# A planned kernel: another price for GpSimd and VectorE at work together, ScalarE allowed to normalise, and two raw float32 tiles instead of four

## The chip, the core and the metric

The kernel runs on one core of one Trainium2 chip. Five engines of that core work in parallel, each through its own instructions in their order: TensorE (PE, matrix products; PEld is its weight load), VectorE (DVE), ScalarE (ACT), GpSimd (POOL) and SyncE (SP, which issues transfers). The metric is the time of one execution in microseconds; the median of the runs counts.

## What is computed

Three stages in a row, float32 in and out (setup and checks left out):

```python
# window attention: batch 2, 8 heads, 576 positions, 64 wide; only the 128 positions up to the own one count
scores = q @ k.T / 8 - slope[head] * distance          # masked outside the window
attn = exp(scores - max); attn = attn / (sum(attn) + 1e-9)
x = (attn @ v).reshape(1152, 512)
# four experts, each token weighted by p = probs / (sum(probs) + 1e-9)
x = sum over e of p[:, e] * (relu(x @ w1[e]) @ w2[e])   # 512 -> 1024 -> 512
# one wide layer
h = relu(x @ w_in); out = (h * h) @ w_out               # 512 -> 2048 -> 512
```

## The kernel before

A float32 product costs TensorE several passes. So the kernel splits an operand into a rounded part and a rest, both in the type float32r, and adds three products: high by high, high by rest, rest by high. Names ending in h hold rounded parts (`qh`, `xh`, `wh`), those ending in l the rests (`ql`, `xl`, `wl`). Rounding runs on ScalarE or VectorE (`rounded`, L519 and L521), the rest is a subtraction on GpSimd or VectorE (`rest`, L525). For a few early tiles the operand is taken raw, as float32, and nothing has to be split: those of the attention's first rows, and in the first expert, for the first 256 tokens, as many of the eight f tiles (128 columns of w1 each) as `RAW1` and `RAW2` say: four for the first product (g1, matmuls `hps<-xfirst,wraw`, L1819) and four for the second (g2, `yacc<-wraw,hfirst`, L1770). Raw inputs are the tiles `xfirst` and `wraw`.

The first part of the program, some 120 us, is not written in an order. Attention and the first expert's work on the first 768 tokens are handed as tasks to a list planner (`Plan`), with the engines that may run each, an estimate of how long it takes, what it waits for, and a due time. `run` takes at each step the task that can start first, or one with an earlier due time that starts within 0.15 us on the same engine, and writes its instructions. That alone sets the order on every engine; the hardware then runs each engine's list strictly in that order. Before, the planner charges for one collision: a VectorE task marked `shared` (roundings and rests out of SBUF) that starts while GpSimd is busy is charged up to twice its length more. A GpSimd task pays nothing.

An attention job is one tile of 128 queries (64 in the last tile) of one head pair. Its steps: `sc` scores on TensorE (L868, L852) from `qh`, `ql` and `khl` (rounded and rest of k), `jo` and `mx` on VectorE (mask, bias and row maximum, L886 and L906), `ex` on ScalarE (exp, L915), `in` on VectorE (one over the row sum, L922 and L926), `no` (multiply the rows by it, `norm`), `tp` on TensorE (transpose, L948, output `tp`, input `ts`), `hi` (copy to `pt`), `ow` and `be` on GpSimd (mask, L969), and for two pairs together `pv` on TensorE (L767, output `xps`). For all but the first rows `no` runs on GpSimd alone, two instructions (one for a tile of 64): L937, `ts<-ts,st`. Jobs are named here by pair and tile in order: A0, A1, B0, B1, C0 and so on. Each TensorE list holds jobs and f tiles mixed; f2 stands for tile 2 of the first product, g2.1 for tile 1 of the second.

Weights of the first expert come in eight pieces (`order`, i = 0 to 7: even for w1, odd for w2, two f tiles each). A piece that is not raw must be split before its first use. A raw piece is split later, for the other tokens. `parted` sets the order of the tasks, `room_` adds waits so that buffers are free. After the planner's part the rest (about 520 us) is written in a fixed order.

Of the kernel before, what the change touches and what calls it, by code (L numbers as in the profile page):

```python
# [12 lines left out]
ACTF = mybir.ActivationFunctionType  # L13
# [24 lines left out]
class Plan:  # L38
# [6 lines left out]
    OTHER = 0.3  # L45
    COLD = 3.0
    WARM = 24.0

    def __init__(self, slots):
        self.tasks = []  # L50
        self.slots = slots
        self.held = {k: [] for k in slots}
        self.at = dict(PE=0.0, ACT=0.0, DVE=0.0, POOL=0.0, SP=0.0)
        self.pool_busy = (0.0, 0.0)

    def add(
        self, name, opts, fn, deps=(), takes=(), bufs=(), due=0.0, follow=(), cold=True,
# [33 lines left out]
    def run(self, until=None):  # L91
        todo = self.tasks
        while todo and not (until and until()):
            cand = []
            for t in todo:
                r = self.ready(t)
                if r is None:
                    continue
                best = None
                for eng, occ, lat in t["opts"]:  # L100
                    start = max(self.at[eng], r)
                    if eng == "PE" and t["cold"] and start < self.COLD:
                        occ, lat = 1.7 * occ, lat + 0.7 * occ
                    if best is None or start + lat + self.OTHER < best[1] + best[3]:
                        best = (eng, start, occ, lat)
                cand.append((best, t))
            assert cand, [t["name"] for t in todo[:20]]
            first, _ = min(cand, key=lambda c: c[0][1])
            eng, start = first[0], first[1]
            (eng, start, occ, lat), t = min(  # L110
                (c for c in cand if c[0][0] == eng and c[0][1] <= start + self.LOOK),
                key=lambda c: c[1]["due"],
            )
            if eng == "DVE" and t["shared"] and self.pool_busy[1] > start:
                more = min(2.0 * occ, self.pool_busy[1] - start)
                occ, lat = occ + more, lat + more
            t["start"], t["end"] = start, start + lat
            self.gap = start - self.at[eng] if start < self.WARM else 0.0
            self.at[eng] = start + occ
            if eng == "POOL":  # L120
                self.pool_busy = (start, start + occ)
            for b in t["takes"]:
                self.held[b.kind].append(b)
            t["fn"](eng)
            for b in t["bufs"]:
                b.users -= 1
                b.end = max(b.end, t["end"])
            todo.remove(t)
# [3 lines left out]
def kernel(  # L132
# [14 lines left out]
    nc = tc.nc  # L147
# [12 lines left out]
    FTQ = FT // NQ  # L160
# [370 lines left out]
    def dve(n, lat=0.05):  # L531
        return ("DVE", 0.15 + 0.00105 * n, 0.15 + 0.00105 * n + lat)
# [289 lines left out]
    def job_tasks(u, i, t, add, b_, end, ready, G, q0, k0, pos, wide):  # L822
# [5 lines left out]
        raw = t == 0  # L828
# [4 lines left out]
        rows, squares = (2 * n, 1) if twin else (n, G)  # L833
        s = {k: Buf(k) for k in ("sc", "ts", "st", "tp")}
        m = n if raw else P
# [5 lines left out]
        def stage(name, opts, fn, lag, **kw):  # L841
            mine[name] = add(key + name, opts, fn, due=end - lag - later, follow=[last.get(name)], **kw)
            return mine[name]
# [84 lines left out]
        def norm(eng):  # L928
            ts, st = s["ts"].tile, s["st"].tile
            if eng == "DVE":  # L930
                nc.vector.tensor_tensor(
                    out=ts[0:rows], in0=ts[0:rows],
                    in1=st[0:rows, 3, 0:squares].unsqueeze(2).to_broadcast([rows, squares, m]), op=ALU.mult,
                )
                return
            for g in range(squares):
                nc.gpsimd.tensor_scalar(  # L937
                    out=ts[0:rows, g, :], in0=ts[0:rows, g, :], scalar1=st[0:rows, 3, g:g + 1],
                    scalar2=1.0, op0=ALU.mult, op1=ALU.mult,
                )  # L940
# [34 lines left out]
        if twin:  # L975
            if "last" not in task:
                task["last"] = plan.add(
                    "last", [("POOL", 2.2, 2.3)], build_last, due=70.0,
                    deps=[task["bias", x, False] for x in range(NP)],
                )  # L980
            tb.append(task["last"])
        us = G * (0.25 if raw else 2 * max(0.107, w * 0.00047))
        tsc = stage("sc", [pe(us)], scores, 7.4, deps=ready,
                    takes=[s["sc"]],
                    bufs=[b_[k] for k in (() if raw else ("qh", "ql", "khl"))])
        if not raw:
            us = 0.15 + 0.00105 * G * n
            tsc = stage("jo", [("DVE", us, us + 0.05)], join, 6.8, deps=[tsc, tb[-1] if twin else t_keep], bufs=[s["sc"]])
        us = G * (0.215 if raw else 0.16 + 0.001 * m)
        tmx = stage("mx", [("DVE", us, us + 0.1)], top, 9.5 if raw else 6.4,  # L990
                    deps=[tsc] + tb, takes=[s["ts"], s["st"]], bufs=[s["sc"]])
# [1 line left out]
                    7.5 if raw else 5.3, deps=[tmx], bufs=[s["ts"], s["st"]])  # L993
        tin = stage("in", [("DVE", 0.33, 0.38)], inv, 3.8, deps=[tex], bufs=[s["st"]])
        us = squares * (0.44 if raw else 0.24 + 0.00085 * m)
        tno = stage("no", [("POOL", us, us + 0.05)] + [dve(G * m)] * raw,
                    norm, 3.4, deps=[tin], bufs=[s["ts"], s["st"]])
        ttp = stage("tp", [pe(squares * 0.108)], turn, 2.4, deps=[tno, task["ident"]],
                    takes=[s["tp"]], bufs=[s["ts"]])
        thi = stage("hi", [act(G * n), dve(G * n)], hi, 2.0, deps=[ttp],  # L1000
# [665 lines left out]

    T0, T1, ITEM = 24.0, 34.0, 4.2

    RAW1, RAW2 = 4, 4

    wtask = {}

# [13 lines left out]
    def weight_parts(i):  # L1686
# [28 lines left out]
        room_ = [task["pv", NP - 1]] if j else []  # L1715
        if j > 1:
            room_ += [wtask["lo", parted[j - 2], 1], wtask.get(("used", parted[j - 2]))]
        if raw and j > PER - (RAW1 + RAW2) // FTQ:
            room_ += [itask["g2", FT - 1]] + [task["evl", u] for u in range(NP)]
        for h in range(2):  # L1720
            a = wtask["hi", i, h] = plan.add(
# [288 lines left out]
```

## Time and profile before

| | us |
|---|---|
| median of 3 runs | 647.51 (647.49 to 647.77) |
| the profiled execution | 648.88 |
| its span, first to last instruction | 646.9 |
| TensorE busy in it | 636.7 (98%) |
| VectorE, GpSimd, ScalarE busy | 467.4 (72%), 393.0 (61%), 295.4 (46%) |
| mean granted clock of TensorE | 0.997 |

The profiled execution took 1.37 us more than the median; 1.98 us of it lie around its span. In a timeline row the first number is the start in microseconds, the second the duration, and a bracket at the end gives the idle time before it and what ended it. Durations of neighbouring matmuls overlap, so a stretch is measured from start to start. "Busy" includes short matmuls on a tile `idle` that are there to occupy TensorE in the first microseconds.

### The profile page before, as it was taken

The numbers are of one execution on the slowest core, as the hardware profiler recorded it, in microseconds if no ns is written. First come the engines' busy times: TensorE is split into PE (matmuls) and PEld (weight loads), VectorE is DVE, ScalarE is ACT, GpSimd is POOL, SyncE is SP. The second block draws the span as 40 slices with busy tenths as digits, with TensorE's granted clock in tenths as the row PEclk, the third lists the DMA queues.
The fourth block names the chain that finished last, engine by engine and source line by source line (L and its number), as shares of the span: only waits on it lengthen the run. The fifth ranks groups of instructions, "written<-read, shape, count | busy, mean of one in ns | idle before, by whom it ended". The sixth has DMA issues, their size and how long they took to land.

```text
span 646.9 us, 11077 instructions
## 1 busy us (share of the span) xinstructions
PE 636.7 (98%) x3929; PEld 570.4 (88%) x3929; DVE 467.4 (72%) x1019; ACT 295.4 (46%) x744; POOL 393.0 (61%) x520
## 2 busy tenths in 40 slices
PE   9999999999999999999999999999999999999997
PEld 8767888899889999899899899899989899898996
DVE  6867967358887877876876876857777667767553
ACT  6867855334444444434434344346554543343230
POOL 2698977339784564565556546247786685665521
PEclk9989999999999999999999999999999999999999
DMA  9953341124125254354443443421114223001012
GB/s 231 275 144 84 81 106 47 39 93 131 34 65 163 82 143 151 93 157 126 119 142 114 130 131 115 130 83 66 33 41 157 81 83 114 16 2 50 1 65 82
DMA packets 46983, 64.70 MB, mean 100 GB/s; under 512 B 6480, under 2 KB 29264, under 8 KB 46928
## 3 DMA queue, kind: packets, MB, share of 16 engines
q1 hardware_dynamic: 35520, 39.48, 20.8%
q10 hardware_dynamic: 11408, 24.51, 12.9%
q8 instruction: 31, 0.51, 0.3%
q14 instruction: 24, 0.20, 0.1%
HBM read 53.23 MB, written 10.75 MB: 99 GB/s over the span
## 4 chain that ended last, share of the span: by engine, by line
PE 94%; POOL 3%; ACT 1%; issue 1%; DMA 0%; DVE 0%; POOLq 0%
PE yacc L1241 38%; PE hps L1150 35%; PE hps L1031 6%; PE yacc L1267 6%; PE sc L868 2%; PE xps L767 1%; PE tp L948 1%; PE hps L1819 1%; POOL ts L937 1%; PE sc L549 1%; POOL pt L969 1%; PE yacc L1770 1%; PE xtp L1333 1%; POOL ql L525 1%; ACT ts L915 0%
## 5 line engine op out<-in xcount | busy, mean ns | idle before, releaser
L1241 PE MATMUL yacc<-wh,hmem 128*128 128x512 f32 x716 | 227.8, 390 | 0.0
L1241 PEld LDWEIGHTS yacc<-wh,hmem 128*128 128x128 f32 x716 | 134.4, 188 | 27.1
L1241 PE MATMUL yacc<-wl,hmem 128*128 128x512 f32 x358 | 139.6, 390 | 0.0
L525 POOL TENSOR_TENSOR wl<-wraw,wh 128x256 fp32r<-128x256 f32 (+1 forms) x80 | 74.7, 958 | 40.8 <-ACT wh L458 29.1
L525 POOL TENSOR_TENSOR hmem<-c,hmem 128x320 fp32r<-128x320 f32 (+1 forms) x64 | 59.2, 943 | 60.3 <-ACT hmem L1181 60.3
L525 POOL TENSOR_TENSOR ls<-wsum,hs 128x256 fp32r<-128x256 f32 x77 | 61.5, 825 | 54.3 <-ACT hs L403 53.6
L1165 DVE TENSOR_TENSOR u<-hps,p 128x256 f32<-128x256 f32 (+1 forms) x80 | 36.4, 455 | 65.2 <-PE hps L1150 63.3
L1161 ACT ACTIVATE p<-hps 128x256 f32<-128x256 f32 (+1 forms) x80 | 32.8, 410 | 108.1 <-PE hps L1150 108.0
L1241 PEld LDWEIGHTS yacc<-wl,hmem 128*128 128x128 f32 x358 | 67.3, 188 | 12.5
L525 POOL TENSOR_TENSOR la<-wraw,ha 128x256 fp32r<-128x256 f32 x54 | 48.6, 919 | 16.8 <-ACT ha L389 16.8
L296 DVE SCALAR_TENSOR_TENSOR wconv<-wraw,wconv 128x512 int32<-128x512 int32 x64 | 57.6, 899 | 1.3
L1185 ACT ACTIVATE hmem<-c 128x256 fp32r<-128x256 f32 (+1 forms) x72 | 31.3, 445 | 53.4 <-DVE c L1165 51.8
L1186 DVE SCALAR_TENSOR_TENSOR hmem<-c,hmem 128x256 fp32r<-128x256 f32 (+1 forms) x72 | 43.3, 623 | 14.0 <-ACT hmem L1185 12.7
L1181 ACT ACTIVATE hmem<-c 128x320 fp32r<-128x320 f32 (+1 forms) x64 | 27.3, 446 | 52.3 <-DVE c L1175 33.5
L1150 PE MATMUL hps<-ht,ls 128*128 128x320 f32 (+1 forms) x160 | 47.5, 297 | 1.3 <-POOL ls L525 1.3
L1150 PE MATMUL hps<-xh,hs 128*128 128x320 f32 (+1 forms) x160 | 47.6, 297 | 0.0
L1150 PE MATMUL hps<-ht,hs 128*128 128x320 f32 (+1 forms) x160 | 47.5, 297 | 0.0
L1150 PE MATMUL hps<-xl,hs 128*128 128x320 f32 (+1 forms) x160 | 47.4, 296 | 0.0
L1150 PE MATMUL hps<-xh,la 128*128 128x320 f32 (+1 forms) x160 | 47.4, 296 | 0.0
L1150 PE MATMUL hps<-lt,hs 128*128 128x320 f32 (+1 forms) x160 | 47.3, 296 | 0.0
L1150 PE MATMUL hps<-xl,ha 128*128 128x320 f32 (+1 forms) x160 | 47.3, 296 | 0.0
L1150 PE MATMUL hps<-xh,ls 128*128 128x320 f32 (+1 forms) x160 | 47.3, 296 | 0.0
(162 smaller groups left out, 1643.6 us busy)
## 6 DMA issues: line engine op xcount, KB each, us to landing
wraw<-in_w_dram SPq DMA_DIRECT2D x32, 512.0 KB, 3.9
wraw<-in_w_out_dram ACTq DMA_DIRECT2D x16, 512.0 KB, 3.9
w<-wconv ACTq DMA_DIRECT2D x32, 256.0 KB, 4.1
wraw<-w SPq DMA_DIRECT2D x16, 512.0 KB, 3.8
wraw<-in_w_in_dram ACTq DMA_DIRECT2D x14, 512.0 KB, 4.1
rq<-in_qT_dram SPq DMA_DIRECT2D x8, 256.0 KB, 7.4
out_dram<-y SPq DMA_DIRECT2D x7, 256.0 KB, 2.1
rk<-in_kT_dram SPq DMA_DIRECT2D x8, 192.0 KB, 4.9
```

What stands on the lines that cost most here:

```text
L296: nc.vector.scalar_tensor_tensor(out=ai, in0=raw[j][:, :, part], scalar=amount, in1=ai, op0=op, op1=ALU.bitwise_or,)
L525: e.tensor_tensor(out=out, in0=in0, in1=f32(in1), op=ALU.subtract)
L868: nc.tensor.matmul(out=sc[0:n, g, :], lhsT=ql[:, qs], rhs=b_["khl"].tile[:, g, j0:j0 + w], start=(ql is b_["qh"].tile), stop=(ql is b_["ql ...
L1031: nc.tensor.matmul(out=ps, lhsT=l_[:, k, cs], rhs=r_[:, k, cols], start=(k == 0 and r_ is xh and l_ is wh and not second), stop=(k == KT - ...
L1150: nc.tensor.matmul(out=ps, lhsT=a[l_][:, k, :], rhs=b[r_][:, k, :], start=start and k == 0 and l_ == r_, stop=stop and k == 1 and l_ == 1, ...
L1161: nc.scalar.activation(out=out, in_=x, func=ACTF.Copy)
L1165: nc.vector.tensor_tensor(out=out, in0=x, in1=y, op=ALU.add)
L1181: nc.scalar.activation(out=hh, in_=r, func=ACTF.Copy)
L1185: nc.scalar.activation(out=hh, in_=src, func=ACTF.Relu)
L1186: nc.vector.scalar_tensor_tensor(out=hl, in0=src, scalar=0.0, in1=f32(hh), op0=ALU.max, op1=ALU.subtract)
L1241: nc.tensor.matmul(out=y, lhsT=l_[:, ns], rhs=r_[:, fo, cols], start=(first and fo == 0 and j == 0), stop=(last and fo == FTQ - 1 and j == 2),
L1267: nc.tensor.matmul(out=y, lhsT=l_[:, ns], rhs=r_[:, fo, :], start=(first and j == 0), stop=(last and j == 2),)
```

## The change

Three edits, and from them a new order of the planned part. First, the planner's collision: GpSimd and VectorE each remember their last task. A GpSimd task that starts before VectorE's last shared task ends is charged 0.65 of the overlap (`HELD`). A shared VectorE task that overlaps GpSimd's is charged 0.3 of the overlap (`SLOWED`), and GpSimd's task is lengthened by 0.65 of it. Second, `norm` may run on ScalarE, as one scaled copy for each square, priced at 0.22 us each. Third, `RAW1` is 2, so that f2 and f3 are made by three float32r products, and piece 2 of the weights is split ahead of them; the wait in `room_` for late raw pieces then applies to none.

```diff
@@ -45,13 +45,15 @@
     OTHER = 0.3
     COLD = 3.0
     WARM = 24.0
+    HELD = 0.65
+    SLOWED = 0.3
 
     def __init__(self, slots):
         self.tasks = []
         self.slots = slots
         self.held = {k: [] for k in slots}
         self.at = dict(PE=0.0, ACT=0.0, DVE=0.0, POOL=0.0, SP=0.0)
-        self.pool_busy = (0.0, 0.0)
+        self.port = dict(POOL=None, DVE=None)
 
     def add(
         self, name, opts, fn, deps=(), takes=(), bufs=(), due=0.0, follow=(), cold=True,
@@ -111,14 +113,23 @@
                 (c for c in cand if c[0][0] == eng and c[0][1] <= start + self.LOOK),
                 key=lambda c: c[1]["due"],
             )
-            if eng == "DVE" and t["shared"] and self.pool_busy[1] > start:
-                more = min(2.0 * occ, self.pool_busy[1] - start)
+            other = self.port["POOL" if eng == "DVE" else "DVE"]
+            if other and (eng == "POOL" or eng == "DVE" and t["shared"]):
+                end = other["start"] + other["occ"]
+                if eng == "POOL":
+                    more = self.HELD * max(end - start, 0.0)
+                else:
+                    both = min(occ, max(end - start, 0.0))
+                    more = self.SLOWED * both
+                    other["occ"] += self.HELD * both
+                    other["end"] += self.HELD * both
+                    self.at["POOL"] = max(self.at["POOL"], other["start"] + other["occ"])
                 occ, lat = occ + more, lat + more
-            t["start"], t["end"] = start, start + lat
+            t["start"], t["end"], t["occ"] = start, start + lat, occ
             self.gap = start - self.at[eng] if start < self.WARM else 0.0
             self.at[eng] = start + occ
-            if eng == "POOL":
-                self.pool_busy = (start, start + occ)
+            if eng == "POOL" or eng == "DVE" and t["shared"]:
+                self.port[eng] = t
             for b in t["takes"]:
                 self.held[b.kind].append(b)
             t["fn"](eng)
@@ -933,6 +944,13 @@
                     in1=st[0:rows, 3, 0:squares].unsqueeze(2).to_broadcast([rows, squares, m]), op=ALU.mult,
                 )
                 return
+            if eng == "ACT":
+                for g in range(squares):
+                    nc.scalar.activation(
+                        out=ts[0:rows, g, :], in_=ts[0:rows, g, :], func=ACTF.Copy,
+                        scale=st[0:rows, 3, g:g + 1],
+                    )
+                return
             for g in range(squares):
                 nc.gpsimd.tensor_scalar(
                     out=ts[0:rows, g, :], in0=ts[0:rows, g, :], scalar1=st[0:rows, 3, g:g + 1],
@@ -993,8 +1011,10 @@
                     7.5 if raw else 5.3, deps=[tmx], bufs=[s["ts"], s["st"]])
         tin = stage("in", [("DVE", 0.33, 0.38)], inv, 3.8, deps=[tex], bufs=[s["st"]])
         us = squares * (0.44 if raw else 0.24 + 0.00085 * m)
-        tno = stage("no", [("POOL", us, us + 0.05)] + [dve(G * m)] * raw,
-                    norm, 3.4, deps=[tin], bufs=[s["ts"], s["st"]])
+        us_act = squares * 0.22
+        tno = stage("no", [("POOL", us, us + 0.05)] + (
+            [dve(G * m)] if raw else [("ACT", us_act, us_act + 0.1)]
+        ), norm, 3.4, deps=[tin], bufs=[s["ts"], s["st"]])
         ttp = stage("tp", [pe(squares * 0.108)], turn, 2.4, deps=[tno, task["ident"]],
                     takes=[s["tp"]], bufs=[s["ts"]])
         thi = stage("hi", [act(G * n), dve(G * n)], hi, 2.0, deps=[ttp],
@@ -1666,7 +1686,7 @@
 
     T0, T1, ITEM = 24.0, 34.0, 4.2
 
-    RAW1, RAW2 = 4, 4
+    RAW1, RAW2 = 2, 4
 
     wtask = {}
 
@@ -1715,7 +1735,7 @@
         room_ = [task["pv", NP - 1]] if j else []
         if j > 1:
             room_ += [wtask["lo", parted[j - 2], 1], wtask.get(("used", parted[j - 2]))]
-        if raw and j > PER - (RAW1 + RAW2) // FTQ:
+        if raw and j > PER - (RAW1 + RAW2) // FTQ + 2:
             room_ += [itask["g2", FT - 1]] + [task["evl", u] for u in range(NP)]
         for h in range(2):
             a = wtask["hi", i, h] = plan.add(
```

The instruction counts move as follows: 20 of the 56 `ts<-ts,st` go from GpSimd to ScalarE, three `ql` and one `khl` (of 384 and 640 columns) from GpSimd to VectorE, 4 copies to `pt` and one `wh` from ScalarE to VectorE; 8 raw matmuls of 256 columns become 24. On every engine the last 230 rows of the order are the same in both kernels.

VectorE at the split of the first x tile, ahead of job A0's mask (names carry buffer numbers; `wraw_335` is weight piece 2), before:

```order
L525 TENSOR_TENSOR khl_368<-rk_286,khl_368 64x768
L525 TENSOR_TENSOR xl_84<-xfirst_344,xh_83 128x256 x3
L525 TENSOR_TENSOR ql_428<-rq_371,qh_416 128x512
L886 COPY_PREDICATED sc_419<-below_105,sc_419 128x2x128
L906 ISA ts_438,st4_102<-sc_419,bias_103 128x128
L906 ISA st4_102 128x1
L906 ISA ts_438,st4_102<-sc_419,bias_103 128x128
L906 ISA st4_102 128x1
L525 TENSOR_TENSOR khl_431<-rk_395,khl_431 64x768
```

And the same place after:

```order
L536 TENSOR_TENSOR khl_368<-rk_286,khl_368 64x768
L536 TENSOR_TENSOR xl_84<-xfirst_344,xh_83 128x256
L532 CAST wh_407<-wraw_335 128x512
L536 TENSOR_TENSOR wl_408<-wraw_335,wh_407 128x512
L536 TENSOR_TENSOR xl_84<-xfirst_344,xh_83 128x256 x2
L897 COPY_PREDICATED sc_424<-below_105,sc_424 128x2x128
L917 ISA ts_441,st4_102<-sc_424,bias_103 128x128
L917 ISA st4_102 128x1
L917 ISA ts_441,st4_102<-sc_424,bias_103 128x128
L917 ISA st4_102 128x1
L536 TENSOR_TENSOR khl_435<-rk_395,khl_435 64x768
```

The split of weight piece 2 (one half's rounding and one rest) has come in ahead of two of the three `xl`, and the `ql` of pair B has left.

GpSimd at the same place, before:

```order
L525 TENSOR_TENSOR xl_84<-xfirst_344,xh_83 128x256
L525 TENSOR_TENSOR ql_393<-rq_268,qh_380 128x512
L937 TENSOR_SCALAR ts_438<-ts_438,st4_102 128x128 x2
L525 TENSOR_TENSOR ql_485<-rq_410,qh_471 128x512
L969 AFFINE_SELECT pt_488<-pt_488 128x2x128 x2
L937 TENSOR_SCALAR ts_466<-ts_466,st0_98 128x128 x2
```

After:

```order
L536 TENSOR_TENSOR xl_84<-xfirst_344,xh_83 128x256
L536 TENSOR_TENSOR ql_386<-rq_268,qh_380 128x512
L536 TENSOR_TENSOR wl_408<-wraw_335,wh_407 128x512
L536 TENSOR_TENSOR ql_445<-rq_371,qh_421 128x512
L955 TENSOR_SCALAR ts_441<-ts_441,st4_102 128x128 x2
L536 TENSOR_TENSOR ql_495<-rq_413,qh_478 128x512
L987 AFFINE_SELECT pt_499<-pt_499 128x2x128 x2
```

The other rest of piece 2 and pair B's `ql` now stand ahead of job A0's normalisation (`ts_438` before, `ts_441` after).

GpSimd from job C1's normalisation (`ts_580`) over D0's (`ts_663`) to D1's (`ts_700`), before:

```order
L937 TENSOR_SCALAR ts_580<-ts_580,st4_102 128x128 x2
L525 TENSOR_TENSOR wl_657<-wraw_575,wh_656 128x512
L937 TENSOR_SCALAR ts_663<-ts_663,st0_98 128x128 x2
L525 TENSOR_TENSOR ql_713<-rq_611,qh_669 128x512
L937 TENSOR_SCALAR ts_700<-ts_700,st1_99 128x128 x2
```

ScalarE after, from pair E's `qh` on, where D0 is `ts_702` and D1 is `ts_749` (two outputs: exp with its row sum; one output: the normalisation):

```order
L530 ACTIVATE qh_705<-rq_644 128x512
L530 ACTIVATE pt_686<-tp_699 128x2x128
L926 ACTIVATE ts_702,st0_98<-ts_702,st0_98 128x128 x2
L1871 ACTIVATE hmem_108<-hps_673 128x256
L530 ACTIVATE khl_728<-rk_657 64x768
L949 ACTIVATE ts_702<-ts_702,st0_98 128x128 x2
L530 ACTIVATE qh_754<-rq_694 128x512
L926 ACTIVATE ts_749,st1_99<-ts_749,st1_99 128x128 x2
L530 ACTIVATE pt_764<-tp_759 128x2x128
L1871 ACTIVATE hmem_108<-hps_732 128x256
L530 ACTIVATE khl_772<-rk_717 64x768
L949 ACTIVATE ts_749<-ts_749,st1_99 128x128 x2
```

The normalisations of D0 and D1 have left GpSimd's list, where a `wl` and a `ql` stood between them, for ScalarE's, where each stands two or three instructions behind its own exp; those of E0 and E1 have moved likewise.

## Rows read from the trace of the kernel before

**Rows 1.** The page: busy time; granted clock in 40 slices (tenths); chain by engine

```profile
PE 636.7 (98%) x3929; PEld 570.4 (88%) x3929; DVE 467.4 (72%) x1019; ACT 295.4 (46%) x744; POOL 393.0 (61%) x520
...
PEclk9989999999999999999999999999999999999999
...
PE 94%; POOL 3%; ACT 1%; issue 1%; DMA 0%; DVE 0%; POOLq 0%
```

**Rows 2.** Stretches: start:end, length, busy PE, PEld, DVE, ACT, POOL; then granted clock

```profile
41.40:43.90 2.50, 0.91 (x7) 0.46 (x5) 2.43 (x5) 1.10 (x4) 2.50 (x4) 0.99 0.62 186
43.80:47.40 3.60, 3.60 (x18) 3.60 (x19) 0.37 (x1) 1.50 (x3) 3.40 (x7) 0.53 0.73 187
24.00:54.00 30.00, 27.66 (x171) 20.42 (x170) 22.19 (x78) 22.63 (x70) 28.26 (x43) 0.94 0.70 180
...
200.00:646.00 446.00, 442.32 (x2591) 400.64 (x2589) 321.19 (x586) 182.25 (x412) 254.10 (x306) 1.00 0.31 95
```

**Rows 3.** Waits of PE from 16 to 126 us: total, times, longest

```profile
PE tp L948 <- POOL ts L937: 3.5, 5, 1.0
```

**Rows 4.** Timeline of PE: the transposes that waited

```profile
42.89 0.33 PE L948 MATMUL tp<-ident,ts 128*128 128x128 f32 x1 [1.02 <-POOL ts L937]
43.78 0.45 PE L948 MATMUL tp<-ident,ts 128*128 128x128 f32 x1 [0.56 <-POOL ts L937]
...
52.82 0.33 PE L948 MATMUL tp<-ident,ts 128*128 128x128 f32 x1 [0.73 <-POOL ts L937]
...
83.03 0.33 PE L948 MATMUL tp<-ident,ts 128*128 128x128 f32 x1 [1.04 <-POOL ts L937]
```

**Rows 5.** Timeline of GpSimd: normalisations and their neighbours

```profile
39.83 0.71 POOL L937 TENSOR_SCALAR ts<-ts,st 128x128 f32<-128x128 f32 x2
40.52 1.26 POOL L525 TENSOR_TENSOR wl<-wraw,wh 128x512 fp32r<-128x512 f32 x1
41.77 1.96 POOL L937 TENSOR_SCALAR ts<-ts,st 128x128 f32<-128x128 f32 x2
...
51.10 1.66 POOL L937 TENSOR_SCALAR ts<-ts,st 128x128 f32<-128x128 f32 x2
```

**Rows 6.** Timeline of VectorE: one pair's khl, alone and beside GpSimd

```profile
33.33 0.95 DVE L525 TENSOR_TENSOR khl<-rk,khl 64x768 fp32r<-64x768 f32 x1
...
40.95 1.65 DVE L525 TENSOR_TENSOR khl<-rk,khl 64x768 fp32r<-64x768 f32 x1
```

**Rows 7.** Timeline of PE: f1 raw, f8 split, what follows each; the last pv

```profile
20.76 1.99 PE L1819 MATMUL hps<-xfirst,wraw 128*128 128x256 f32 x8
22.40 0.47 PE L868 MATMUL sc<-khl,qh 128*128 128x256 f32 x1
...
23.31 0.47 PE L868 MATMUL sc<-khl,qh 128*128 128x256 f32 x1
...
56.75 0.28 PE L1031 MATMUL hps<-xh,wh 128*128 128x256 f32 x1
...
58.19 0.38 PE L948 MATMUL tp<-ident,ts 128*128 128x128 f32 x2
...
124.49 1.54 PE L767 MATMUL xps<-pt,rv 128*64 128x128 f32 x24
```

**Rows 8.** Timelines of VectorE and GpSimd: rests of 512 columns

```profile
30.10 0.68 DVE L525 TENSOR_TENSOR wl<-wraw,wh 128x512 fp32r<-128x512 f32 x1
...
17.31 2.04 POOL L525 TENSOR_TENSOR ql<-rq,qh 128x512 fp32r<-128x512 f32 x1 [0.36 <-DVE qh L521]
```

**Rows 9.** SyncE: issue of weight pieces 1 and 2; pieces' time to landing

```profile
7.86 1.10 SPq L216 DMA_DIRECT2D wraw<-in_w_dram  x2
...
DMA to landing us min/median/max: 5.4/7.1/10.0
```

**Rows 10.** ScalarE: an exp (timeline); a plain copy (its line, durations in ns)

```profile
24.53 0.39 ACT L915 ACTIVATE ts<-ts,st 128x128 f32<-128x128 f32 x1
...
L606 ACT ACTIVATE bias<-rel x6: 293/293/309, 3.5 to 4.5; 128x128 bf16<-128x128 f32 x6
```

## The prediction

> **What bounds the kernel now.** I read the page first: TensorE is busy for 98% of the span, and 94% of the chain that ended last is its own [rows 1]. So the end moves by what TensorE's work shrinks, and by what it waits less or at a higher clock. The stretches come next. From 200 us on TensorE is busy in 442.3 of 446 us, and nothing of the order there changes [rows 2]; later stages follow the planned part by a shift. In the planned part it is busy in only 0.91 of the 2.50 us from 41.4 on, and then works for 3.6 us at a granted clock of 0.53 [rows 2]: the lower of its two levels, 1.2 instead of 2.4 GHz, nearly throughout. The slice around it is the only one below 9 tenths [rows 1]. The waits name the cause: five transposes, 3.5 us in sum, waited for GpSimd's normalisation [rows 3]. The timeline places them: two squares of job D0 (1.02 and 0.56), one of E0 (0.73), a late tile at 83 us (1.04) [rows 4]; the fifth is the remainder. GpSimd was the late engine: busy 28.26 of the 30 us up to 54, while VectorE had 22.2 and ScalarE 22.6 [rows 2]. And it was late partly through a collision. D0's pair took 1.96 us and E0's 1.66, and both are of the same shape as the pair before D0's, which took 0.71 [rows 5]. VectorE shows the other half: khl of one shape takes 0.95 us alone and 1.65 beside a wl of GpSimd that began first and ended at 41.78; 41.78 to 42.60 is 0.82 us [rows 5, 6]. So one engine stands still until the other's instruction is through.
>
> **Raw tiles.** f1 took 22.40 - 20.76 = 1.64 us raw; a split tile, f8, 58.19 - 56.75 = 1.44 us [rows 7]. Two tiles change: 2 x 0.20 = 0.40 us less on TensorE, all of it on the path. The rest of the TensorE work is the same, only in another order.
>
> **What has to be ready for it.** Piece 2's split now comes before f2. Its transfer is the second of two issued from 7.86 us; at the largest time to landing, 10.0 us from about 8.4, it lands at 18.4 [rows 9]. That is just ahead of its rounding, which the order puts on ScalarE and VectorE behind work that ended near 18.6. No cost, and 0.3 us if the transfer is later by as much. The rests are the dearer part. From 19.35 us, the end of GpSimd's first ql [rows 8], both engines read two SBUF operands at once: VectorE one wl (0.68), two xl (256 columns each, together as much as the wl, an estimate), one khl (0.95); GpSimd a wl and pair B's ql of the same size (1.26 each) [rows 5, 6, 8]. In the old order GpSimd was idle here, and pair B's ql ran on VectorE. If only one engine moves at a time, these come to 0.68 + 0.68 + 0.95 + 2.52 = 4.83 us, and the last is done at 24.2. B0's scores need pair B's khl and ql; they started at 23.31 [rows 7], and stand in the new order one third product behind A1's, at about the same time. That is a wait of 0.9 us. The bounds are 0 (the two engines never meet: VectorE's rests alone end at 21.7, GpSimd's at 21.9) and 1.6 (one more collision of the size of khl's, 1.65 - 0.95 = 0.70). I take 0.9, since the rows show full blocking.
>
> The Trainium skill (SBUF — State Buffer, section "Who interferes with whom") says that a VectorE instruction with two SBUF inputs and a reading GpSimd instruction exclude each other for a whole instruction; the khl row agrees with its 0.82 us behind GpSimd's end. The planner's new price (0.65 and 0.3 of the overlap) is milder: by it nothing would wait here, by the rule 0.9 us.
>
> **Normalisation on ScalarE.** Twenty of 56 instructions leave GpSimd, about 0.36 us each undisturbed. D0's and E0's are among them, and so are D1's and E1's. On ScalarE one costs between 0.29 us (a plain copy of 128x128) and 0.39 (an exp, with two numbers for each row of the tile where the normalisation has one) [rows 10]. I take 0.35, 0.7 us a pair, against 1.96 and 1.66. ScalarE has room: 7.4 of 30 us are idle up to 54 [rows 2], and twelve of its 20 new instructions (B1, C0, D0, D1, E0, E1), 4.2 us, fall there. So D0's and E0's waits go: 1.02 + 0.56 + 0.73 = 2.31 us. What is late next stands in ScalarE's list. D1's normalisation follows D1's exp, a copy to pt, a ReLU and a khl. I count that TensorE comes to D1's transpose within 0.1 us of it, and to those of E0 and E1, four in a row behind the second pv, likewise. I charge 0.4 us for the two places, between 0 and 2.3 (as much as left).
>
> **The clock.** Without the 1.6 us of idle time at 42 the stretch at half clock has no cause in sight: (1 - 0.53) x 3.6 = 1.69 us come back [rows 2]. No slice behind 49 us shows a lower clock, though E0's wait and the one at 83 us lie there [rows 1, 4], so I take no new one for the 0.9 us at 23. The waits at 76 and 83 us, 1.2 us together, I leave in: all eight pieces are split earlier in the new order, so GpSimd has no wl there any more, but the places of twenty other waits are new. Bounds: 0 and 1.2 us of gain.
>
> Later waits are not moved: the last attention job, the loads behind it and the expert stages keep their order, and shift.
>
> **Sum.** -0.40 + 0.9 - 2.31 + 0.4 - 1.69 = -3.1 us. The profiled execution gives 648.88 - 3.1 = 645.8. It is 1.37 us above the median, and I carry the difference over: 647.51 - 3.1 = **644.4 us**.
>
> **Rivals.**
>
> *All waits go.* VectorE and GpSimd never meet at 20 us, ScalarE is never late, 76 and 83 us are clear: -0.40 - 2.31 - 1.69 - 1.19 = -5.6, 641.9 us. For it: GpSimd loses 20 x 0.36 = 7.2 us of normalising. Against it: the khl row, by which the two engines do meet.
>
> *The waits move to ScalarE.* A transpose of D1 or E0 waits as long as D0's did, and the clock falls as it did at 43.8. Then only the raw tiles and the wait at 23 us count: -0.4 + 0.9 = +0.5, 648.0 us. For it: ScalarE is a strict list too, with exps, copies and ReLUs between a row sum and its use. Against it: no exp or copy there is stretched by another engine as GpSimd's are. The Trainium skill (ScalarE: Activation LUTs, "Rules for kernel authors") speaks for this rival: multiplications belong on VectorE, not on ScalarE.
>
> *The half clock was in the profiled execution alone.* It was 1.37 us slower than the median, near to the 1.69. Then 1.69 us of the gain do not exist in the timed runs: -1.4, 646.1 us.
>
> *Slower.* At 20 us GpSimd and VectorE alternate in the worst way: they collide once more, pair B's khl is done at 24.9, TensorE idles 1.6 us and then works for the next 3.6 us at half clock as it did after 43.8, 1.7 us more [rows 2]; all jobs are later against the f tiles, and transposes wait elsewhere what they waited at 42. That is -0.4 + 1.6 + 1.7 = +2.9, 650.4 us. It decides where khl is done at 24.9 or later, so that TensorE stands idle as long as D0 made it. Against it: half of that wait is what the blocking rows give.
>
> That ScalarE is merely allowed and never chosen is ruled out by the order.
>
> **Chances.** The forecast, 643 to 646, 0.48; all waits gone 0.12; the clock only in the profile 0.12; moved to ScalarE 0.17; slower 0.11. A difference of 0.2%, 1.3 us, is about what can be told from no change here. The first two are faster by more, the third lies on the edge and is halved: 0.66 faster, 0.23 the same, 0.11 slower. The range that leaves out two in ten reaches from the best case to just above the ScalarE one: 641.9 to 648.2.
>
> **What would show it.** In the changed profile: f2 and f3 as 24 products of about 0.12 us; a wait of B0's scores near 23.4 us for khl or ql, of 0.5 to 1.2 us; no wait of D0's and E0's transposes for GpSimd; in the waits of TensorE, fewer than 2 us for GpSimd's `ts` and under 0.6 us for ScalarE's; a granted clock of 9 tenths or more in every slice behind 24 us; the last pv (124.5 us before [rows 7]) some 3 us earlier, and all later waits where they were. Wrong would be the step on the clock if half clock shows again anywhere up to 60 us; the step at 20 us if B0's scores wait not at all or over 1.6 us; the shift if the last pv is 3 us earlier and the end is not.

## The result and the profile after

The kernel after takes **642.44 us** (median of 6 runs, 642.06 to 643.04) against 647.58 us before (6 runs, 647.49 to 647.9) on the same chip: 0.992 of the time, with a 95% interval of 0.9907 to 0.9933, or 5.1 us less. The forecast was 644.4, in a range of 641.9 to 648.2: the sign was right, the gain is 2 us larger than the sum, and the time lies just below the 643 to 646 that had the largest chance. The profiled execution of after took 642.18 us, with a span of 640.5.

The page of after, the lines that answer to [rows 1]:

```profile
PE 631.9 (99%) x3937; PEld 568.2 (89%) x3937; DVE 472.6 (74%) x1028; ACT 298.8 (47%) x759; POOL 381.4 (60%) x496
...
PEclk9999999999999999999999999999999999999999
...
PE 95%; DVE 1%; ACT 1%; DMA 1%; issue 0%; POOL 0%; SPq 0%
```

GpSimd is at 0% of the chain that ended last, and no slice of the clock is below 9 tenths. The stretches, as in [rows 2] (busy PE, PEld, DVE, ACT, POOL, then the granted clock):

```profile
24.00:54.00 30.00, 28.65 (x202) 22.77 (x203) 26.56 (x95) 27.69 (x91) 21.64 (x32) 1.00 0.71 183
200.00:640.00 440.00, 435.96 (x2561) 395.42 (x2559) 317.05 (x577) 179.67 (x408) 252.82 (x303) 1.00 0.30 94
```

GpSimd is busy for 21.64 of the 30 us instead of 28.26, ScalarE for 27.69 instead of 22.63. All the waits of TensorE's matmuls from 16 to 126 us, to be read beside [rows 3]:

```profile
PE sc L879 <- DVE khl L536: 1.1, 1, 1.1
PE hps L1051 <- ACT hfirst L1773: 0.5, 1, 0.5
PE hps L1839 <- ACT xfirst L530: 0.3, 1, 0.3
PE hps L1839 <- ACT hfirst L1773: 0.2, 1, 0.2
```

No transpose is among them. The largest is new and stands where the forecast put it: B0's scores wait for pair B's khl. The timelines of TensorE, VectorE and GpSimd there, against [rows 6 to 8]:

```profile
24.87 0.36 PE L879 MATMUL sc<-khl,qh 128*128 128x256 f32 x1 [1.08 <-DVE khl L536]
...
19.35 0.68 DVE L536 TENSOR_TENSOR wl<-wraw,wh 128x512 fp32r<-128x512 f32 x1
19.95 2.91 DVE L536 TENSOR_TENSOR xl<-xfirst,xh 128x256 fp32r<-128x256 f32 x2
...
23.78 0.95 DVE L536 TENSOR_TENSOR khl<-rk,khl 64x768 fp32r<-64x768 f32 x1
...
19.51 1.66 POOL L536 TENSOR_TENSOR wl<-wraw,wh 128x512 fp32r<-128x512 f32 x1 [0.70 <-DVE wh L532]
21.13 1.45 POOL L536 TENSOR_TENSOR ql<-rq,qh 128x512 fp32r<-128x512 f32 x1
```

The two xl, together as large as the wl that takes 0.68 us, last 2.91 us: the second ends (22.86) just behind the ql on GpSimd (22.58). Then come job A0's mask and maximum (to 23.78), and only then khl.

[Rows 3] are the waits of the matmuls. The weight loads (PEld) have rows and waits of their own, which the prediction did not use. The weight loads' waits for a normalisation, first of before from 24 to 126 us, then of after from 16 to 126:

```profile
PEld tp L948 <- POOL ts L937: 6.4, 13, 1.3
```

```profile
PEld tp L966 <- POOL ts L955: 0.2, 1, 0.2
PEld tp L966 <- ACT ts L949: 0.2, 1, 0.2
```

So by the weight loads the transposes waited 6.4 us in 13 places, not 3.5 in five, and nearly all of that is gone. A weight load can wait while TensorE still works on products, so such a sum need not be lost time; here it goes with the span. All waits of weight loads from 16 to 126 us add up to 13.7 us in a second profile of before (span 646.2), 11.5 with ScalarE alone (643.1), 9.7 in after (640.5) and 9.0 with the price alone (640.3), all four at a full clock. The last pv starts at 117.92 us, 6.57 earlier than in [rows 7], the span is 6.4 shorter, and everything behind the last pv has shifted, to within 0.2 us. The table compares profiled executions.

| part of the difference | forecast, us | between the profiles, us |
|---|---|---|
| two raw tiles | -0.40 | -0.40 (taken over) |
| waits of transposes | -2.31 + 0.4 | -6.0 (weight loads, 6.4 to 0.4) |
| half clock at 43.8 us | -1.69 | -1.69 |
| new waits at the front | +0.9 | +2.1 (the four rows above) |
| sum | -3.1 | -6.0; the spans differ by 6.4 |

The table takes the transposes from the weight loads and the front from the matmuls; with all waits of weight loads on both sides (13.35 and 9.71 us) the sum is -5.7, with those of matmuls alone -3.5. The timed runs differ by 5.1, not 6.4. The first experiment shows why; the others ask which part of the change brought it.

### The profile page after: what moved, and what is told of

It is laid out like the page before. It is cut to its first block, busy times and chain, and to the rows that moved or that the text cites. A ratio compares the mean times of both kernels' runs of the same rounds, so it can differ in the third digit from the quotient of the medians.

```text
span 640.5 us, 11076 instructions
## 1 busy us (share of the span) xinstructions
PE 631.9 (99%) x3937; PEld 568.2 (89%) x3937; DVE 472.6 (74%) x1028; ACT 298.8 (47%) x759; POOL 381.4 (60%) x496
## 4 chain that ended last, share of the span: by engine, by line
PE 95%; DVE 1%; ACT 1%; DMA 1%; issue 0%; POOL 0%; SPq 0%
PE yacc L1261 38%; PE hps L1170 35%; PE hps L1051 8%; PE yacc L1287 7%; PE xps L778 2%; PE sc L879 2%; PE tp L966 1%; PE yacc L1790 1%; DMA first<-in_qT_dram 1%; DVE xl L536 1%; PE xtp L1353 1%; PE sc L863 1%; ACT ts L926 0%; PE sc L871 0%; ACT pt L530 0%
```

## The experiments

The theory at the start was that of the forecast: ScalarE's normalising frees TensorE's transposes, the price only shuffles, the raw tiles cost a little. The rivals: the price carries the gain; the raw tiles do.

**The kernel before, once more.** No edit.

> The kernel before, unchanged. It asks one thing: does the half clock at 43.8 us belong to every execution, or to the profiled one alone? 3.6 us at a clock of 0.53 lower the mean of the span by (1 - 0.53) x 3.6 / 647 = 0.0026. If it belongs to the kernel, every timed execution shows a mean clock near 0.997, and a second profile shows the half clock again near 44 us. If it was in the profiled execution alone, the timed executions show 0.999 to 1.000, and a profile with the half clock is some 1.4 to 1.7 us longer than they. Time 647.5.

The result is neither of the two: some executions have it. Of 55 executions of before in these comparisons, 17 show a mean clock of 0.997 and take 649.03 us (median; 648.18 to 649.46), the other 38 show 0.999 or 1.0 and take 647.69 (646.99 to 649.07). The mean of 0.997 is what 3.6 us at 0.53 gives; where the clock fell was seen in one profiled execution alone, the one that the forecast was read from. The two groups lie 1.34 us apart. That all of it is the clock is not shown: the second profile has a full clock and more waits, and one execution at a full clock took 649.07. The second profile (span 646.2) lacks the half clock. Its page, then the two stretches of [rows 2], then the weight loads' waits:

```profile
PEclk9999999999999999999999999999999999999999
```

```profile
41.40:43.90 2.50, 1.46 (x12) 0.84 (x9) 2.43 (x4) 1.40 (x6) 2.50 (x4) 1.00 0.63 182
43.80:47.40 3.60, 3.60 (x23) 2.67 (x22) 2.16 (x9) 2.59 (x6) 3.46 (x7) 1.00 0.69 182
```

```profile
PEld tp L948 <- POOL ts L937: 7.0, 15, 1.6
```

D0 waits here for one square only, TensorE works for 1.46 instead of 0.91 us of the first stretch, and the clock stays whole. The median before hardly contains the half clock, so the forecast's 1.69 us were not there to be won against it. All the other kernels here showed 0.999 or 1.0 in every run; 647.7 us is the mark for them.

**D0's and E0's normalisations alone on ScalarE**, in the order of before (u is the pair, 7 and 8 are D and E; i is the tile; lines around it left out):

```diff
+            if i == 0 and u in (7, 8):
+                for g in range(squares):
+                    nc.scalar.activation(
+                        out=ts[0:rows, g, :], in_=ts[0:rows, g, :], func=ACTF.Copy,
+                        scale=st[0:rows, 3, g:g + 1],
+                    )
                 return
```

> The kernel before with its order, except that the normalisations of jobs D0 and E0 are written for ScalarE, at the place they had in the program; nothing is planned anew. My theory (TensorE's transposes waited for GpSimd's normalisations): the waits of D0 and E0 go, 2.31 us by TensorE's rows and 2.9 by the rows of its weight loads (1.26, 0.75, 0.92), and 1.7 more if the half clock is in every execution: 643.0 to 645.3. The rival that only the new prices, by their other order, bring the gain: no change, 647.5. The rival that the waits move: D1 and E1 or the second pv wait instead, 647 to 647.5, and the profile shows them there.

645.56 us (645.12 to 646.25), ratio 0.9967 (0.9955 to 0.998), 0.3 us above my range, which had room for the clock. The weight loads' waits for GpSimd fall from 7.0 to 4.1 us, with 0.4 for ScalarE:

```profile
PEld tp L955 <- POOL ts L944: 4.1, 12, 1.2
PEld tp L955 <- ACT ts L938: 0.4, 2, 0.3
```

Two moved pairs are worth 2.1 us: the forecast's -2.31 for these two waits holds.

**One part of the change at a time.** ScalarE allowed; two raw tiles; the new price. Each is the kernel before with that part of the diff alone.

> The kernel before with ScalarE allowed to normalise; the old price of a shared access and four raw tiles stay. My theory: most of the 6.4 us for which the weight loads of the transposes waited go, half a clock less or not, and B0's scores do not wait since piece 2 is split late: 640.5 to 643.5. The rival that the new price carries the gain: GpSimd and VectorE still collide as before, 646 to 647.5. The rival that the raw tiles carry it: 647.5.

> The kernel before with two raw tiles instead of four; old price, all normalisations of pairs on GpSimd. My theory: 0.4 us less work, 1.1 to 1.8 us of new waits ahead of B0's scores near 24 us, and the transposes wait for GpSimd about as before: 647.5 to 649.5. The rival that the raw tiles carry the gain, by taking piece 2's split out of the crowded part at 40 us: 642.5 to 645.

> The kernel before with the new price of a shared access alone; four raw tiles, all normalisations of pairs on GpSimd. If GpSimd simply has too much to do ahead of the transposes, a truer price only shuffles it: 646.8 to 648.3, with 5 us or more of waits of the weight loads. If the price carries the part that ScalarE alone did not bring: 645, with under 4 us of such waits.

| kernel | us (range) | ratio to before (interval) | weight loads wait for a normalisation on GpSimd, us |
|---|---|---|---|
| ScalarE alone | 645.15 (644.79 to 645.53) | 0.9958 (0.9946 to 0.9971) | 3.6 |
| raw tiles alone | 648.05 (646.88 to 648.77) | 0.9999 (0.999 to 1.0008) | 6.3 |
| price alone | 642.34 (642.16 to 642.95) | 0.9912 (0.9895 to 0.9929) | 1.3 |
| all three (after) | 642.44 (642.06 to 643.04) | 0.992 (0.9907 to 0.9933) | 0.2 |

**My theory fell here.** The price alone gives what all three give (645 was the better of its two forecasts), with every pair's normalisation still on GpSimd; ScalarE alone gives half, and misses my range. With ScalarE allowed and the old price D0 is still on GpSimd, and its wait is longer than any of before. The weight loads of the kernel with ScalarE alone, their waits and then the timeline row:

```profile
PEld tp L955 <- POOL ts L944: 3.6, 6, 2.4
```

```profile
42.74 0.14 PEld L955 LDWEIGHTS tp<-ident,ts 128*128 128x128 f32 x1 [2.38 <-POOL ts L944]
```

With the price alone two more waits of the transposes' weight loads, 1.0 us, are put down to a `ql` and a mask on GpSimd, so 2.3 us for GpSimd in all. With two raw tiles alone the time is that of before, but B0's scores did not wait, where I had written 1.1 to 1.8 us; 1.6 us of waits for ScalarE's copies (`xfirst`, `hfirst`) came instead.

**Two parts at a time**: after without ScalarE's right; after with four raw tiles.

```diff
-        tno = stage("no", [("POOL", us, us + 0.05)] + (
-            [dve(G * m)] if raw else [("ACT", us_act, us_act + 0.1)]
-        ), norm, 3.4, deps=[tin], bufs=[s["ts"], s["st"]])
+        tno = stage("no", [("POOL", us, us + 0.05)] + [dve(G * m)] * raw,
+                    norm, 3.4, deps=[tin], bufs=[s["ts"], s["st"]])
```

> The kernel after without ScalarE's right to normalise: new price and two raw tiles alone. If ScalarE's normalising is the gain: the transposes wait for GpSimd again, some 6 us by the weight-load rows of before, and B0's scores still wait 1.1 us at 24 us: 647 to 649. If the price carries what ScalarE alone did not bring (it measured 2.6 of the 5.1 us): 644.5 to 645.5, with under 4 us of waits of the weight loads for GpSimd's normalisation.

```diff
-    RAW1, RAW2 = 2, 4
+    RAW1, RAW2 = 4, 4
```

> The kernel after with four raw tiles: price and ScalarE's normalising together. My theory: the waits ahead of B0's scores, 1.08 us for khl and 0.75 for ScalarE's copies, go, since piece 2 is split late again; 0.4 us of raw work comes back: 642.4 - 1.8 + 0.4 = 641.0. If the raw tiles' gain is instead that piece 2's rest is out of GpSimd's crowded list at 40 us: the transposes of D0 or E0 wait again, 1 to 3 us, 643 to 645. If it is worth nothing either way, as alone: 642.4.

Without ScalarE: 643.59 us (643.41 to 643.93), 0.993 (0.9915 to 0.9945); the weight loads wait 1.2 us for GpSimd's normalisations. With four raw tiles: **641.45 us** (641.06 to 642.01), 0.9897 (0.9882 to 0.9912), the lowest time of all. The first lies below both of its ranges, the second near its 641.0. Beside a given price, ScalarE brings 0.9 us (642.34 to 641.45) or 1.15 (643.59 to 642.44), and the two raw tiles fewer *cost* 1.0 (641.45 to 642.44) or 1.25 (642.34 to 643.59): 0.4 us less work against 2.1 us of waits at the front, where 0.5 us of waits is left with four. With four raw tiles the front is clean. The stretch from 24 to 54 us, then the one wait of the matmuls from 16 to 126 us:

```profile
24.00:54.00 30.00, 30.00 (x201) 23.34 (x201) 27.74 (x96) 28.98 (x93) 26.80 (x37) 1.00 0.66 176
```

```profile
61.14 0.62 PE L966 MATMUL tp<-ident,ts 128*128 128x128 f32 x2 [0.54 <-ACT ts L949]
```

**What in the price does it?** It changes two things: GpSimd is now charged for VectorE's accesses (0.65), and VectorE pays 0.3 of an overlap instead of the whole rest. The first run strikes GpSimd's charge out of the price; the second keeps the old price and only raises the planner's durations of GpSimd's work to the means that the trace of before shows.

```diff
-    HELD = 0.65
+    HELD = 0.0
```

> The new price alone, as in the run that had nothing else, but with GpSimd's own charge struck out (0 instead of 0.65); VectorE still pays 0.3 of an overlap instead of the old full rest. If it is GpSimd's charge that makes the order fit: the transposes wait as before, 646 to 648. If it is that VectorE no longer pays too much for an overlap, and so takes more rests from GpSimd: 642 to 643.5.

```diff
-        return ("POOL", 0.2 + 0.0021 * n, 0.2 + 0.0021 * n + lat)
+        return ("POOL", 0.2 + 0.00235 * n, 0.2 + 0.00235 * n + lat)
...
-        us = squares * (0.44 if raw else 0.24 + 0.00085 * m)
+        us = squares * (0.55 if raw else 0.35 + 0.00085 * m)
...
-        us = 0.2 + 0.00085 * G * n
+        us = 0.27 + 0.00085 * G * n
```

> The kernel before with its old price of a shared access; only the planner's durations of GpSimd's work are raised to the means of the trace before: 1.40 us for a rest of 512 (1.28 planned), 0.92 for a pair's normalisation (0.70), 0.49 for a mask step (0.42). Nothing is said there of who disturbs whom. Theory of lateness (the price helps since it makes the planner expect GpSimd as late as it is, so that TensorE's list has other work until a transpose is due): most of the gain comes with the means too, 642.5 to 644.5, with under 2.5 us of waits of the weight loads for GpSimd's normalisation. Theory of avoidance (the price helps since single collisions are planned around): the means don't know where a collision falls, D0 or another pair is late again by 1 us or more, 645.5 to 648.

Without the charge: 647.13 us (646.66 to 649.64), 0.9988 (0.9978 to 0.9998): nearly all of the gain is gone. With the means: 643.92 us (643.77 to 645.0), 0.994 (0.9926 to 0.9953): 3.8 of 5.4 us, without a word on contention. The weight loads' waits, then the stretch from 24 to 54 us, without the charge:

```profile
PEld tp L966 <- POOL ts L955: 4.8, 16, 0.8
```

```profile
24.00:54.00 30.00, 28.44 (x181) 20.68 (x180) 23.45 (x83) 22.72 (x72) 29.27 (x44) 1.00 0.71 178
```

with the means:

```profile
PEld tp L948 <- POOL ts L937: 2.1, 7, 0.6
```

```profile
24.00:54.00 30.00, 29.61 (x195) 22.63 (x193) 24.62 (x83) 23.25 (x74) 29.27 (x44) 1.00 0.68 174
```

and with the whole price:

```profile
PEld tp L966 <- POOL ts L955: 1.3, 5, 0.3
```

```profile
24.00:54.00 30.00, 29.45 (x195) 22.36 (x194) 27.37 (x92) 26.14 (x82) 27.99 (x45) 1.00 0.77 178
```

GpSimd is hardly freer in the good ones: 29.27 of 30 us busy with the means, exactly as without the charge, and 27.99 with the whole price, against the 28.26 of [rows 2]. What differs is whether it is late against the list. The planner's code gives each task a start, in the same order as the lists are written; the traces give the real start. Lateness below is real minus planned, less that of job A0, the first pair (0.44, 0.12, 0.10 and 0.03 us from left to right: the spans don't begin alike).

| normalisation | before, planned and real | price without the charge | before with the means | price alone |
|---|---|---|---|---|
| D0 | 40.15, 41.77: **+1.2** | 41.83, 43.13: **+1.2** | 40.92, 40.79: **-0.2** | 39.75, 39.05: **-0.7** |
| E0 | 47.13, 51.10: **+3.5** | 49.16, 51.86: **+2.6** | 50.38, 50.32: **-0.2** | 50.06, 48.98: **-1.1** |

The rows of GpSimd for the two new columns that differ most, without the charge and with the means:

```profile
43.13 1.96 POOL L955 TENSOR_SCALAR ts<-ts,st 128x128 f32<-128x128 f32 x2
...
51.86 0.72 POOL L955 TENSOR_SCALAR ts<-ts,st 128x128 f32<-128x128 f32 x2
```

```profile
40.79 1.43 POOL L937 TENSOR_SCALAR ts<-ts,st 128x128 f32<-128x128 f32 x2
...
50.32 2.57 POOL L937 TENSOR_SCALAR ts<-ts,st 128x128 f32<-128x128 f32 x4
```

With the price alone, GpSimd's normalisations and then TensorE's transposes (four in a row: C1's and D0's, then E0's and E1's), which start without a wait:

```profile
39.05 0.72 POOL L955 TENSOR_SCALAR ts<-ts,st 128x128 f32<-128x128 f32 x2
...
48.98 1.42 POOL L955 TENSOR_SCALAR ts<-ts,st 128x128 f32<-128x128 f32 x4
...
40.77 0.66 PE L966 MATMUL tp<-ident,ts 128*128 128x128 f32 x4
...
52.73 0.66 PE L966 MATMUL tp<-ident,ts 128*128 128x128 f32 x4
```

It is not these two jobs alone. Of the eleven normalisations from A1 to F1, before is late by 0.0 to 4.4 us, growing, and without the charge by 0.3 to 3.1; with the means they lie between -0.7 and +0.8, with the price alone between -1.5 and -0.1. The other two kernels that keep the pairs on GpSimd agree: raw tiles alone (no gain) has D0 +1.3 and E0 +2.3 (less 1.03 for A0), after without ScalarE (a gain) -0.4 and -0.6 (less 2.35).

This is the cause, as far as these runs go. Before, the planner believed GpSimd faster than it was; TensorE's list came to D0's and E0's transposes when the plan, not GpSimd, had them ready. Believe GpSimd slower, by the charge or by plain means, and the lists change in two ways. Ahead of E0's transposes TensorE gets more of its other tasks: four more with the means, five with the price alone, two without the charge. Ahead of D0's normalisation GpSimd gets fewer rests: seven before, six with the means, four with the price alone, so that it comes at 40.79 and 39.05 us instead of 41.77; the rests that left run on VectorE. TensorE's list ahead of D0's transposes has one task more with the means and none with the price. So the price alone clears D0 by GpSimd's list, and E0 by both: there GpSimd comes 2.1 us earlier, and TensorE has the five tasks first.

No run changes one of the two lists alone. The last 1.6 us between the means (643.92) and the price alone (642.34) may be collisions that the price steers around, or rests that it gives to VectorE (27.37 us busy against 24.62); the runs don't tell these apart. And each of these kernels is one order: how far a time moves when the planner's durations change for no reason was not measured.

**The front.** A price of full exclusion, which the rows there suggest:

```diff
-    HELD = 0.65
-    SLOWED = 0.3
+    HELD = 1.0
+    SLOWED = 1.0
```

> The kernel after with the price of a full exclusion, 1.0 and 1.0 instead of 0.65 and 0.3: the planner then gives ScalarE more normalisations and GpSimd one of A1's x rests at 20 us. If the rows' full blocking is what the planner lacks: B0's scores wait 0.5 us or less and nothing else comes, 641.3 to 642. If the blocking is unavoidable in a crowded front: the same as after, 642.1 to 643. A third way, that moving the order brings new waits elsewhere: 643 to 645.

641.74 us (641.5 to 642.15), 0.9902 (0.9887 to 0.9916): B0's wait is gone, and the one wait of the matmuls left from 16 to 126 us is 0.49 us of a transpose. With four raw tiles too (the two diffs together):

> Four raw tiles, ScalarE may normalise, and the price of a full exclusion (1.0 and 1.0): what each measured singly, 1.0 us less by the raw tiles and 0.7 us less by the price, against the kernel after at 642.4. If they add: 640.7. If both remove the same waits at the front, as the rows suggest (B0's 1.08 us goes in either): 641.2 to 641.6. If the order gets a new wait: over 642.

641.86 us (641.44 to 642.11), 0.9902 (0.9888 to 0.9916): they don't add, and B0's wait is in none of the three kernels. This one, the full price alone and four raw tiles alone cannot be told from each other; all three are 0.6 to 1.0 us below after.

Last, one instruction moved in after, nothing planned anew (u 5 is pair B):

```diff
-            rest(eng, b_["ql"].tile, b_["rq"].tile, b_["qh"].tile)
+            rest("DVE" if u == 5 else eng, b_["ql"].tile, b_["rq"].tile, b_["qh"].tile)
```

> The kernel after with one instruction moved: pair B's ql at 21.13 us is written for VectorE, ahead of khl, at the place it has in the program; nothing is planned anew. If GpSimd's two rests hold VectorE's two x rests by a whole exclusion (2.91 us for two that need about 0.7): the x rests are through when the wl on GpSimd is, near 21.2 us, in 1.9 us instead of 2.91; ql then costs VectorE 0.7, khl is done about 0.3 us earlier, and B0's scores wait 0.8 us instead of 1.08: 642.1. If VectorE's own order or another engine holds them: 2.9 us as before, khl 0.7 us later, 643.1.

The timelines of VectorE and GpSimd there, then TensorE's wait:

```profile
20.21 0.68 DVE L536 TENSOR_TENSOR wl<-wraw,wh 128x512 fp32r<-128x512 f32 x1
20.82 1.83 DVE L536 TENSOR_TENSOR xl<-xfirst,xh 128x256 fp32r<-128x256 f32 x2
...
24.16 0.95 DVE L536 TENSOR_TENSOR khl<-rk,khl 64x768 fp32r<-64x768 f32 x1
...
20.37 1.65 POOL L536 TENSOR_TENSOR wl<-wraw,wh 128x512 fp32r<-128x512 f32 x1 [0.70 <-DVE wh L532]
...
25.26 0.36 PE L879 MATMUL sc<-khl,qh 128*128 128x256 f32 x1 [1.12 <-DVE khl L536]
```

The two xl take 1.83 instead of 2.91 us as soon as no ql on GpSimd follows the wl: it held them. They now end 0.63 us behind the wl on GpSimd (22.02). From the wl's start to khl's end it is 4.90 us instead of 5.38. The wait is not the 0.8 us that I had written, since the wl began 0.5 us later against TensorE's f1 (1.11 us ahead of it at 21.32, where in after it was 1.62 ahead of 20.97). 642.0 us (641.61 to 642.66), 0.9906 (0.9892 to 0.992): not to be told from after. The Trainium skill (SBUF — State Buffer, "Who interferes with whom") states the exclusion for whole instructions; the 2.91 and 1.83 us agree.

## Why the prediction was right, and where it was wrong

**Sign and range: right**, and for the reason on which most of it rested: the transposes' waits for GpSimd's normalisations. D0's and E0's are worth 2.1 us when moved alone, against -2.31 in the sum. But 642.44 is not in the 643 to 646 that had 0.48; it is nearest to the rival by which all waits go (641.9, 0.12). Of that rival the waits did go, while VectorE and GpSimd did meet.

**Who takes the waits away: wrong.** The step "On ScalarE one costs between 0.29 us [...] and 0.39 [...] So D0's and E0's waits go" gave the credit to ScalarE, and the price got none. ScalarE alone brings 2.6 us, the price alone 5.4. I read the price only as "milder" than the blocking in the rows, and asked whether the engines would still collide; what mattered is whether the plan expects GpSimd as late as it comes. The planner's own starts told it: E0's normalisation stands at 47.13 us in the plan and at 51.10 in its row.

**Size of the waits: the mis-sized term.** -2.31 for two jobs and two more waits left in; measured are 6.4 us in 13 places by the weight loads, 6.0 of them gone. The waits at 76 and 83 us went too, and the small ones of 0.2 to 0.3 us, which the matmuls' rows don't show. The sum comes near the span with the weight loads' rows (-6.0, or -5.7 with all of them, against 6.4), not with [rows 3] (with its 3.5 it would be -3.5).

**The normalisation on ScalarE: right in price, wrong in cost.** The pair takes what was forecast (0.7), as a timeline row of after shows:

```profile
31.39 0.69 ACT L949 ACTIVATE ts<-ts,st 128x128 f32<-128x128 f32 x2
```

The +0.4 for waits behind ScalarE's list did not come: 0.2 us in one place. The rival by which the waits move to ScalarE fell with it: beside the new price ScalarE's share is a gain of 0.9 to 1.15 us. The Trainium skill's rule (ScalarE: Activation LUTs, "Rules for kernel authors") that multiplications belong on VectorE, not on ScalarE, is not tested by this: ScalarE took them from GpSimd, and no run here gave a pair's normalisation to VectorE.

**The front: right in mechanism, short in sum.** +0.9 for B0's scores; 1.08 measured, and that they are so near is in part luck. The sum of one engine at a time had the two engines through at 24.2 us with khl as the last. The other rests were through at 22.86; A0's mask and maximum, which stand ahead of khl on VectorE and were not in the sum, took 0.92 us more, and khl ended at 24.73. Also not seen: three products of the first layer waited 0.47, 0.28 and 0.23 us for ScalarE's copies (`hfirst`, `xfirst`). The copy behind the 0.28 stands after the rounding of piece 2, which waited 0.40 us for its transfer, where I had written "No cost, and 0.3 us if the transfer is later by as much":

```profile
18.61 0.63 ACT L530 ACTIVATE wh<-wraw 128x512 fp32r<-128x512 f32 x1 [0.40 <-DMA wraw<-in_w_dram]
```

So the raw tiles, which the forecast had at +0.5 in sum, cost 1.0 to 1.25.

**The clock: wrong against the median.** -1.69 was read from one execution, and 17 of 55 show the lower mean clock. I had named the case (the half clock in the profiled execution alone, 646.1 us) with a chance of 0.12. That the sum is off by no more than 2 us is luck: this error (1.7 too much) and the front's (1.2 too little) stand against the waits (some 4 too little). Without a clock term, and with the 7.0 us of waits of the second profile, -0.40 + 2.1 - 6.6 is -4.9, against 5.1 measured.

**The shift: right.** The end moved by 6.4 us, the last pv by 6.57; "some 3 us" was the size of the sum.

## What to carry to other kernels

Where a list is planned by a table of durations, compare the planned starts with the trace's before touching the work: an engine that the planner believes too fast makes others wait though its load is bearable, and measured means in the table may already give most of the gain. Read the waits of weight loads beside those of matmuls. A clock seen in one profiled execution is a term of the sum only if the timed runs show it too.

## What the runs showed of the hardware

The same program, unchanged, ran at a mean granted clock of 0.997 in 17 of 55 executions and at 0.999 or 1.0 in 38. In one profile 3.6 us are at 0.53, the lower of the two levels for nearly all of the stretch, in the other at 1.00. The two profiles differ ahead of the place by whether TensorE waited there for one square of D0 or for two: it was busy 1.46 or 0.91 of 2.50 us. The kernel with two raw tiles alone likewise has two groups of times, 646.88 to 647.13 (5 runs) and 648.05 to 648.77 (6 runs), all at a clock of 0.999 or 1.0; what parts these is open.

Two `xl` on VectorE, 256 columns each, took 2.91 us beside a wl and a ql on GpSimd and 1.83 beside the wl alone; GpSimd's own wl took 1.66 us behind a wl on VectorE that had begun first, against 1.26 in [rows 5].
